# One small weight load of an attention and feed-forward kernel: the queue it is issued on, and how its second copy is made

## The chip, the cores and the metric

The kernel runs on one core of a Trainium2 chip. A core has five engines with instruction queues of their own: TensorE (matrix products, PE in the profile; PEld are its weight loads), VectorE (DVE), ScalarE (ACT), GpSimd (POOL) and SyncE (SP), which here only issues transfers. Transfers (DMAs) can be issued from SP, from ScalarE and from GpSimd, and are carried out by 16 DMA engines that the core has in common for all of them. The metric is the time of one execution on the device, in microseconds. Before the change the median of three runs is 282.02 us (280.19 to 282.04).

## The reference

Two layers follow each other. The first is a linear attention with a feature map of exponentials, over 8 batches of 8 heads, 576 tokens and 64 channels per head:

```python
def phi(x):
    proj = np.einsum('bhsd,df->bhsf', x, w_phi)          # w_phi: 64 x 128
    proj = proj - np.max(np.abs(proj), axis=-1, keepdims=True)
    return np.concatenate([np.exp(proj), np.exp(-proj)], axis=-1)
q_p, k_p = (phi(q), phi(k))
kv = np.einsum('bhsf,bhsd->bhfd', k_p, v)
z = np.sum(k_p, axis=2)
num = np.einsum('bhsf,bhfd->bhsd', q_p, kv)
den = np.einsum('bhsf,bhf->bhs', q_p, z)[..., None] + 1e-06
attn = (num / den)
```

The second takes the attention's result as 4608 tokens of 512 channels and computes `max(x @ w1, x @ w2, x @ w3) @ w_out`, with three 512 x 768 matrices and one of 768 x 512. The result is 4608 x 512 in float32.

## The kernel before

**Units and chunks.** The attention is done in 16 units of four heads each (`attention(u)`), the feed-forward layer in eight chunks of 512 tokens and a last one for the remaining 64 tokens of each batch (`chunk`). The chunks of the early batches run among the units of the later ones, so that all engines have work from both layers at the same time.

**One unit.** The queries and keys of a unit come in as bf16 `qk_bf`, most of them by transfers that GpSimd issues and that convert on the way (L439, L455). For unit 0 the keys come in float32 as `k_raw` in two halves, issued by SP (L449), and are converted on chip: the first half by VectorE, the second by GpSimd (L452). The last 64 queries of each head come as `q_tail` (L370) and are converted by GpSimd (L468). In the first four units TensorE transposes these tiles into PSUM (`tps`, L483) and VectorE or ScalarE copies them into `qkT` (L499, L501); later units use a transposing transfer (L508). In `qkT` two tokens' channels share the 128 rows: rows 0 to 63 belong to the even tile, rows 64 to 127 to the odd one. Then the projections follow: `psk` and `psq` (L536), `pst` for the tails (L557) and `psm` with the roles exchanged (L631). Each of them uses 64 of the 128 rows, once the upper and once the lower ones, and so w_phi must stand in both halves of the rows: that is the tile `wph` (bf16, 128 x 128). VectorE takes the maxima of the projections (L525), ScalarE the exponentials (L522, L582), GpSimd multiplies the values by exponentials (`vab`, L590), TensorE makes the products `kvps` (L611) and `psn` (L663), VectorE and GpSimd divide (L666 to L673), and the result is transposed into `xT`.

**Loading w_phi.** One transfer reads w_phi twice and fills all 128 rows of the float32 tile `wphi_f` (L400). SP issues it, between the two halves of the first keys. One VectorE instruction then converts `wphi_f` to `wph` (L408). Every projection of every unit depends on this conversion; the first of them is `psk` of unit 0.

**The order of the work.** Nothing is scheduled by the compiler: each piece of work is a `node`, with the engines that may run it and its assumed cost, and the long text PLAN gives for each node its number, engine (T TensorE, D VectorE, A ScalarE, G GpSimd, S SP), the numbers of the buffers that it opens, and a start time. `plan` (L246) reads the text. The instructions of each engine are emitted in the order of these starts; each engine works through its own list in order and waits at an instruction until what it needs is there. The start times are not enforced on the chip. The nodes that matter below are: 1 the constant tile for fillers, 2 the load of w_phi, 3 its conversion, 6 and 8 the two loads of the first keys, 7 and 9 their conversions, 10 and 180 loads of tails, 11 the first load of v, 13, 17 and 15 the first transposes, 14 ScalarE's copy of the first of them, 23 the first `psk`, 64 the first `psm`, 1546 ScalarE's load of its function table.

**Fillers.** Where PLAN leaves TensorE a gap early in the kernel, `fill` (L264 to L285) puts products of a constant tile in (`idler`, L866), whose results nobody reads. For each TensorE node it looks at the gap to the end of the one before. If the gap is over 0.35 us it emits a filler at 0.1 us after that end (at the very beginning at 0.65, when the constant tile is ready), and further ones in steps of 0.43 us while the time is up to 4.6 us, then of 0.26, as long as the time stays below the node's start less 0.8 us (less 0.2 us once it is past 4.6). Each needs a free PSUM bank. With the starts of before this gives 14 fillers, seven of them ahead of node 13 and none between nodes 13 and 23.

Of the kernel before, what the change touches and what calls it, by code (L numbers as in the profile page):

```python
# [8 lines left out]
FP32 = mybir.dt.float32  # L9
# [7 lines left out]
DF = 128  # L17
# [69 lines left out]
19T0@7.9 99G@7.9 1150G@8.1 333S0@8.3 34A@8.3 20D@8.4 21T1@8.5 31D@8.7 66A@8.8 1148G@8.9 68A@9.3 36D@9.3 40T06@9.5  # L87
38A@9.8 22D@9.9 41D@10.2 65A@10.3 43T4100@10.3 50A0@10.8 32D@10.8 47A@11.0 51G0@11.1 37A@11.2 102T0@11.3 42D@11.4
44A@11.7 69T52@11.9 35A@12.0 103D1@12.1 52G@12.2 71A@12.5 49D@12.7 123T103@12.8 72A@13.0 46D@13.0 53G@13.3 124D@13.4
54A@13.5 256G0@13.5 48A@13.7 100T6@13.8 125D@14.0 57A@14.0 70A@14.1 104T7@14.3 1149G@14.3 58T001@14.5 101D@14.6  # L90
73A@14.6 45A@15.1 113T53@15.1 56G@15.1 105D@15.2 106T2611@15.3 60A@15.4 59A@15.5 115D@15.6 116T74@15.6 74A0@15.7
126T1011@15.8 110A@15.9 114D@16.2 55G@16.2 128A@16.3 120A@16.6 119D@16.8 111A@17.1 183G@17.3 109D@17.4 61T53@17.5
255G@17.5 121A@17.6 112D@18.0 117A@18.1 332G1@18.3 63A@18.6 122D@18.6 133A0@18.7 75T63@18.9 62A@18.9 118A@19.1
135G0@19.1 132D@19.2 184T5@19.2 129D@19.5 107A@19.6 78T47@19.7 76D0@19.9 137A@20.1 134G@20.2 108A@20.3 185D0@20.3
188T6@20.5 189A@20.8 79D@20.9 147T2511@21.1 136A@21.1 127A@21.2 140G@21.3 77D@21.3 186T6@21.4 130A@21.5 405G3@21.5
331G@21.8 80D@21.8 149A@21.8 83T14@21.9 187D@22.2 131A@22.3 141T137@22.3 335G@22.5 148A@22.6 139G@22.8 84D1@22.8
197T060@23.0 142A@23.2 81D0@23.2 1159T2@23.3 150A@23.3 198D@23.4 157A1@23.8 138G@23.9 86T31@23.9 151A@24.0 199D@24.0
1161T6@24.2 143A@24.5 87D@24.6 1160A0@24.7 1157T7@24.8 259G@25.0 85D@25.1 82G0@25.2 88D@25.5 144T30@25.5 1162A@25.6
1158D@25.9 207T12@26.1 152T45@26.3 402G@26.4 146A@26.5 209D@26.6 145A@26.6 161T67@26.7 155A@26.8 158T03@27.0 89D0@27.2
154A@27.3 162D0@27.3 1169T2@27.3 90G@27.5 159D@27.8 153A@27.9 181D0@28.2 163D@28.3 156A@28.4 182S@28.4 160D@28.7  # L100
403G@28.7 224T0400@28.7 1170A@28.9 166T57@29.1 164D0@29.3 169T63@29.4 228A@29.4 165G1@29.6 167D1@29.6 1167T2@29.7
226A@29.9 208D@30.1 225A@30.5 170D@30.7 1153G@30.8 93T5@31.0 168D@31.1 1168A@31.3 91T6@31.3 171D@31.5 200T7011@31.7
227A@31.8 92D@31.9 190T12@32.0 205A@32.3 174T3@32.3 172D0@32.3 196D@32.5 1163T64@32.6 192A@32.7 173G@32.9 94D@33.1
202A@33.2 175D@33.5 195A@33.7 260T5@33.9 257D@33.9 206D@34.0 1151G@34.1 258S@34.2 191A@34.2 176T4@34.4 261D1@34.6
1165T3@34.7 1164A@34.7 194A@35.2 193D@35.3 201A@35.7 177D@35.9 210T1211@36.1 204A@36.1 1152G@36.2 266T16500@36.3
203D@36.3 1173T4@36.6 214A@36.6 272D@36.9 215A@37.1 264T7@37.5 216D@37.5 1183T0@37.6 270A@37.7 213D@37.9 268A@38.1
1174D0@38.2 1156G@38.3 1181T2@38.4 212A@38.6 269D@38.8 217A0@38.9 265A@39.1 1177T4@39.3 1166D@39.4 211A@39.4 267A@39.7
1184D@40.0 271A@40.2 286T3100@40.3 219G0@40.4 276T67@40.5 1178D@40.6 1182A@40.7 1193T0@40.8 287A@41.2 292D@41.2
234A1@41.4 282D@41.6 277A@41.6 262T2@41.7 1175T4@42.1 220A@42.1 1194D@42.2 288A@42.2 218G@42.5 278A@42.5 289D@42.8
1195T0@43.0 291A@43.0 263D@43.1 281A@43.3 279D@43.8 1179T5@43.9 280A@43.9 336S2@44.0 1196D@44.4 290A@44.4 1155G@44.6  # L110
1176A@44.7 300T7611@44.8 1180D@45.0 273T12@45.1 221T103@45.3 301A@45.3 274D@45.6 293A0@45.8 302A@46.0 275D@46.2
296A1@46.5 283T15@46.5 304A@46.6 294G@46.7 229T74@46.7 285D@47.0 1191T2@47.0 222A@47.1 232A@47.4 284D@47.6 223A@47.8
1189T5@47.9 233A@48.1 1192D@48.2 303A@48.6 295G@48.7 238T43@48.8 474S1@48.9 1190D@49.0 230A@49.1 235T21@49.1
305T60@49.5 239D1@49.6 231A@49.7 1197T5@49.8 236D@50.1 406S1@50.2 309A@50.2 240D@50.5 246T74@50.7 1154G@50.8 308A@50.8
237D@50.9 243T23@51.1 247D0@51.3 306A@51.3 297T001@51.5 244D@51.7 307A@52.0 248D@52.2 310A1@52.4 245D@52.6
371T2600@52.7 376T47@52.9 241D0@53.0 1171G@53.1 249D1@53.2 372A@53.2 1185T3@53.2 298D@53.3 299A@53.6 374A@53.9
404S0@54.1 1187T1@54.1 472G1@54.1 1186D@54.3 373A@54.4 334S@54.7 250G1@54.8 375A@54.9 1205T0@55.0 1188D@55.2
475S1@55.3 380A@55.4 322T63@55.8 378A@55.9 609S0@55.9 242G@56.1 319T12@56.2 379A@56.3 323D0@56.4 1206T@56.5 377A@56.8
320D@56.8 324D@57.3 473G@57.3 321D@57.7 314T41@57.8 541G3@58.0 1207A0@58.0 337T13600@58.2 315D1@58.4 311T27@58.5
339A@58.7 325D0@58.8 253T0@58.9 326G0@59.1 312D@59.1 342A@59.2 1198T@59.2 316D@59.5 254A@59.7 313D@60.0 543G@60.3  # L120
343D@60.4 476G@60.5 357T7200@60.6 424T040@60.8 317D0@61.0 361A@61.0 1201T1@61.1 360D@61.1 318G@61.3 1199A1@61.3
425D@61.5 338A@61.8 1202T@62.0 363D@62.1 341A@62.3 426D@62.4 1493G@62.5 359A@62.8 340D@63.0 362A@63.1 251T0@63.3
540G@63.3 358A@63.4 327T2@63.6 1203A2@63.6 252D@63.8 329T3@63.9 328A@64.2 344T76@64.3 330D@64.4 354T01@64.5 477S0@64.7
347T45@64.7 346D@64.9 1223T3@65.1 348A@65.2 345D@65.5 349A@65.9 1213T2@65.9 353D@66.1 1224A1@66.3 350D@66.7
1215T7@66.8 351A@66.8 355D@67.3 364A0@67.4 1214A@67.6 1225T4@67.7 366G1@67.8 356D@67.9 352A@68.1 367A@68.6
407T6011@68.6 1216A@68.7 1226D@68.8 427T1511@68.9 417T23@69.1 431A@69.3 1235T7@69.4 413D@69.4 429A@69.6 365G@69.9
422A@69.9 433D@70.0 1221T4@70.3 428A@70.4 420D@70.4 1200S@70.4 432A@70.6 381A1@70.9 430D@71.0 1204S@71.0 419A@71.1
1217T5@71.1 423D@71.3 1208S@71.6 412A@71.6 410D@71.9 611G0@72.0 1227T1@72.0 418A@72.1 744S1@72.2 608G@72.2 1236D@72.5
1218A@72.6 1233T2@72.9 1494G@72.9 1222A@73.1 1228D@73.1 542S@73.4 421A@73.6 1229T7@73.7 1234D@74.0 544S2@74.1
434A0@74.1 411A@74.3 436G0@74.4 414T31@74.7 408A@74.8 1230D@74.9 446T0211@74.9 368T045@75.2 448A@75.4 415D@75.5  # L130
# [158 lines left out]
def kernel(  # L289
# [109 lines left out]
    def phi_load(n_):  # L399
        queue_of[n_.eng].dma_start(wphi_f, w_phi.unsqueeze(0).to_broadcast([2, D, DF]))  # L400
# [497 lines left out]
```

## Time and profile before

| | |
|---|---|
| median of three runs | 282.02 us (280.19 to 282.04) |
| the profiled execution | 282.44 us |
| its span | 280.6 us |
| TensorE busy | 268.6 us, 96% of the span, 3460 products |
| VectorE busy | 224.0 us, 80% |
| ScalarE busy | 197.7 us, 70% |
| GpSimd busy | 161.3 us, 57% |
| moved by DMA | 43.24 MB |

The span goes from the first to the last instruction that the profiler recorded; the time of the execution is 1.84 us longer. Times in the rows count from the start of the span. A row of the view in order of time gives the start, the duration, the engine, the line, the operation, what it writes and reads, how many instructions are merged into the row, and in brackets how long the engine stood idle before it and what it waited for. A row of the chain of waits gives the start, the duration and what the end of the kernel hung on during it. In the rows of DMA issues the last number is the time from issue to landing. The rows of a DMA queue give packets, MB and the time of their packets as a share of the 16 engines; q1 is SP's queue, q0 GpSimd's, q10 ScalarE's.

### The profile page before, as it was taken

Reading aid. Unit: us, or ns where it says so; the run is one execution under the profiler, and the core shown is the slowest. Engines: PE = TensorE matmul, PEld = TensorE weight load, DVE = VectorE, ACT = ScalarE, POOL = GpSimd, SP = SyncE. Lnnn points to the kernel's source line nnn. Section 1 sums busy time; section 2 is a strip of 40 time slices with the busy share of each in tenths; the row PEclk is TensorE's granted clock in tenths of the full one; section 3 lists DMA queues with packets and bytes.
Section 4 is the critical chain, followed back from the end, with each engine's and each line's share of the span. In section 5 each row is a group of like instructions: output and inputs, shape, how many; then the busy total and the mean of one; then the engine's idle time right before and its main releaser. Section 6 shows DMA issues by size and latency. Waiting matters only on the chain.

```text
span 280.6 us, 8449 instructions
## 1 busy us (share of the span) xinstructions
PE 268.6 (96%) x3460; PEld 150.2 (54%) x3460; DVE 224.0 (80%) x452; ACT 197.7 (70%) x488; POOL 161.3 (57%) x158
## 2 busy tenths in 40 slices
PE   5788999999999999999999999999999999999994
PEld 1457654765465546555564466445654664444451
DVE  1798999979988899998987999978998994375530
ACT  2699999988998999999376997689969850200001
POOL 6599899996795693666575483339345753000000
PEclk9997999999999999999999999999999999999998
DMA  7999999199999799997969979499444015200054
GB/s 146 238 236 208 208 247 199 34 304 168 227 187 191 140 201 267 194 189 88 224 100 233 181 127 242 65 252 174 96 85 161 2 24 147 77 0 0 2 146 153
DMA packets 70632, 43.24 MB, mean 154 GB/s; under 512 B 47042, under 2 KB 61762, under 8 KB 70594
## 3 DMA queue, kind: packets, MB, share of 16 engines
q1 hardware_dynamic: 55602, 30.91, 48.5%
q0 software_dynamic: 14912, 11.77, 28.7%
q8 instruction: 27, 0.44, 0.6%
q14 instruction: 11, 0.09, 0.1%
q10 hardware_dynamic: 80, 0.03, 0.0%
HBM read 34.67 MB, written 9.44 MB: 157 GB/s over the span
## 4 chain that ended last, share of the span: by engine, by line
PE 87%; DVE 4%; ACT 3%; DMA 2%; POOL 1%; issue 1%; SPq 0%; DVEq 0%
PE ups L713 34%; PE ops L746 17%; PE ops L741 11%; PE psn L663 7%; PE kvps L611 6%; PE psk L536 3%; PE psm L631 3%; PE psq L536 3%; DMA wphi_f<-in_w_phi_dram 2%; DVE m L525 2%; ACT Ek L522 1%; PE pst L557 1%; PE tps L483 1%; PE pxT L683 1%; POOL x_sb L673 1%
## 5 line engine op out<-in xcount | busy, mean ns | idle before, releaser
L713 PE MATMUL ups<-xT,w_bf 128*128 128x512 bf16 x432 | 100.7, 379 | 0.6 <-issue 0.5
L590 POOL TENSOR_TENSOR vab<-v_raw,em 128x1152 bf16<-128x1152 f32 (+1 forms) x36 | 67.9, 1903 | 22.3 <-ACT em L582 21.5
L522 ACT ACTIVATE Ek<-psk 128x512 bf16<-128x512 f32 x128 | 72.5, 625 | 5.0 <-PE psk L536 4.4
L522 ACT ACTIVATE Eq<-psm 128x512 bf16<-128x512 f32 x128 | 71.7, 626 | 4.5 <-PE psm L631 4.3
L713 PEld LDWEIGHTS <-w_bf 128*128 128x128 bf16 x432 | 39.4, 98 | 46.4 <-issue 2.3
L673 POOL TENSOR_TENSOR x_sb<-y,rden 128x640 bf16<-128x640 f32 x32 | 39.9, 1253 | 33.0 <-DVE rden L671 28.9
L746 PE MATMUL ops<-wout_bf,hT 128*128 128x512 bf16 (+2 forms) x222 | 51.4, 374 | 0.0
L721 ACT ACTIVATE hT<-ups 128x512 bf16<-128x512 f32 x34 | 20.6, 618 | 37.4 <-PE ups L713 37.4
L525 DVE TENSOR_REDUCE m<-psk 128x4 f32<-128x512 f32 x64 | 42.7, 681 | 3.3 <-PE psk L536 2.0
L719 DVE TENSOR_TENSOR hT<-hT,ups 128x512 bf16<-128x512 bf16 x54 | 36.0, 680 | 8.8 <-PE ups L713 8.0
L525 DVE TENSOR_REDUCE m<-psq 128x4 f32<-128x512 f32 x64 | 41.6, 679 | 0.7 <-PE psq L536 0.6
L666 DVE TENSOR_TENSOR y<-psn,sq 128x325 f32<-128x325 f32 x64 | 29.9, 486 | 3.4 <-PE psn L663 1.9
L746 PEld LDWEIGHTS <-hT 128*128 128x128 bf16 x222 | 20.4, 98 | 22.4 <-issue 0.3
L669 DVE TENSOR_TENSOR y<-y,psn 128x325 f32<-128x325 f32 x64 | 29.2, 485 | 1.0
L663 PEld LDWEIGHTS <-Eq 128*128 128x128 bf16 x512 | 23.3, 99 | 10.5 <-issue 1.8
L522 ACT ACTIVATE Et<-pst 128x256 bf16<-128x256 f32 x64 | 24.0, 409 | 3.0 <-PE pst L557 2.6
L663 PE MATMUL psn<-kv_sb,Eq 128*128 128x65 bf16 x512 | 25.2, 195 | 0.9 <-DVE m L525 0.6
L755 DVE COPY osb<-ops 128x512 f32<-128x512 f32 (+1 forms) x22 | 14.7, 669 | 12.7 <-PE ops L746 12.7
L741 PE MATMUL ops<-xT 128*128 128x512 bf16 x96 | 24.5, 379 | 0.0
L755 ACT COPY osb<-ops 128x512 f32<-128x512 f32 (+1 forms) x15 | 8.9, 593 | 20.8 <-PE ops L746 13.3
L536 PEld LDWEIGHTS <-qkT 64*128 64x128 bf16 x512 | 16.4, 96 | 11.6 <-issue 8.4
L611 PE MATMUL kvps<-vab,Ek 64*128 64x65 bf16 x1024 | 20.5, 191 | 0.7 <-POOL vab L590 0.7
(71 smaller groups left out, 313.5 us busy)
## 6 DMA issues: line engine op xcount, KB each, us to landing
v_raw<-in_v_dram SPq DMA_DIRECT2D x16, 576.0 KB, 6.8
out_dram<-osb SPq DMA_DIRECT2D x32, 256.0 KB, 3.8
qk_bf<-in_k_dram POOLq DMA_DIRECT2D x15, 288.0 KB, 7.4
qk_bf<-in_q_dram POOLq DMA_DIRECT2D x15, 256.0 KB, 7.8
w_bf<-in_moe_w_dram POOLq DMA_DIRECT2D x3, 768.0 KB, 19.1
q_tail<-in_q_dram SPq DMA_DIRECT2D x16, 64.0 KB, 6.1
wout_bf<-in_moe_w_out_dram POOLq DMA_DIRECT2D x1, 768.0 KB, 15.6
out_dram<-osb SPq DMA_DIRECT2D x6, 128.0 KB, 2.4
```

The costliest lines, as they stand in the source:

```text
L522: nc.scalar.activation(out, ps, EXP, scale=1.0 - 2.0 * s)
L525: nc.vector.tensor_reduce(out, ps, AXX, ALU.max, apply_absolute_value=True)
L536: nc.tensor.matmul(pss[par]()[:, i, :], lhsT=qkT()[r, block(c, h * HB + i), :], rhs=wph[r, :], start=True, stop=True)
L590: made.append(any_of(n_, lambda n_, g=g, t0=t0, t1=t1: (nc.vector if n_.eng == "DVE" else nc.gpsimd).tensor_tensor(vab()[:, g, t0:t1, 0:D] ...
L611: nc.tensor.matmul(kvps[ab]()[:, pr, g, :], lhsT=Ek[g]()[r, t, :] if t < MT else Et[g]()[r, 0, t - MT, :], rhs=vab()[r, g, t, :], start=(p ...
L663: nc.tensor.matmul(psn[g]()[:, c, :], lhsT=Eq[g]()[:, t0:t0 + P] if c < 4 else Et[g]()[:, 1, pr, :], rhs=kv()[:, pr, ab, g, :], start=True ...
L666: n_ = nd("xu", {"DVE": 0.42}, lambda pr=pr, ab=ab, psn=psn, y=y: nc.vector.tensor_tensor(y()[:, ab], psn[0](), sq()[:, 2 * pr + ab, :].un ...
L673: divs.append([any_of(n_, lambda n_, pr=pr, y=y, rden=rden: (nc.vector if n_.eng == "DVE" else nc.gpsimd).tensor_tensor(x_sb()[:, pr].rear ...
L713: nc.tensor.matmul(ups(), lhsT=w_bf[i + 1][:, ct, j * P:(j + 1) * P], rhs=tokens_of(ct), start=(ct == 0), stop=(ct == CT - 1))
L719: nc.vector.tensor_tensor(hT()[:, j, :], hT()[:, j, :], ups(), ALU.max)
L741: nc.tensor.matmul(ops_()[:, 0:width], lhsT=tile_of(ct, tt), rhs=line_w[c_i > MOVE][:, ct, cols], start=(ct == 0), stop=False)
L746: nc.tensor.matmul(ops_()[:, 0:width], lhsT=hT()[:, j, tt * P:(tt + 1) * P], rhs=wout_bf[:, j, cols], start=False, stop=(j == JT - 1))
```

## The change

The tile `wphi_f` has 64 rows instead of 128, and the transfer reads w_phi once, without a broadcast. ScalarE issues it, ahead of its table load; SP's list loses it, so the second half of the first keys follows the first half directly. VectorE converts `wphi_f` twice, once into rows 0 to 63 of `wph` and once into rows 64 to 127, as one node. PLAN is written anew: the order of the nodes on VectorE, GpSimd and TensorE stays the same as before, on SP and ScalarE it differs in the moved load alone. The starts differ by some tenths of a microsecond, and PSUM bank numbers are in part others. Of 920 buffer openings 23 follow another earlier user than before. The fillers follow from the new starts.

```diff
 PLAN = """
-1D@0.3 1546A@0.7 6S0@0.7 4G0@1.2 2S@1.3 8S@1.9 5G@2.0 10S0@2.5 95G1@2.7 7D@3.4 0G@3.5 11S0@3.8 96G@4.0 13T0@4.2
-180S1@4.4 14A0@4.6 179G2@4.8 3D@4.8 23T00100@5.3 9G@5.5 29D@5.8 24A@5.8 17T2@5.9 178G@6.1 15T3@6.3 18D@6.4 25A@6.4
-97D@6.7 16D@6.8 64T2400@6.9 1147G@6.9 28A@6.9 98S@7.0 26D@7.1 33T35@7.3 67A@7.4 30T67@7.5 12G@7.7 39D@7.8 27A@7.9
...
+1D@0.3 2A@0.7 6S0@0.7 4G0@1.2 1546A@1.3 8S@1.3 10S0@1.9 5G@2.0 95G1@2.7 11S0@3.2 0G@3.5 7D@3.8 180S1@3.8 96G@4.0
+3D@4.3 13T0@4.5 179G2@4.8 14A0@5.0 9G@5.5 23T00100@5.6 17T2@5.9 29D@6.1 24A@6.1 178G@6.1 15T3@6.3 18D@6.7 25A@6.7
+1147G@6.9 97D@7.0 16D@7.1 64T2400@7.2 28A@7.2 98S@7.3 26D@7.5 33T35@7.6 12G@7.7 67A@7.7 30T67@7.9 99G@7.9 39D@8.1
+1150G@8.1 27A@8.2 19T0@8.2 333S0@8.3 34A@8.7 20D@8.7 21T1@8.8 1148G@8.9 31D@9.1 66A@9.1 68A@9.6 36D@9.7 40T06@9.8
...
-    wphi_f = const.tile([P, DF], FP32, name="wphi_f")
+    wphi_f = const.tile([D, DF], FP32, name="wphi_f")
...
     def phi_load(n_):
-        queue_of[n_.eng].dma_start(wphi_f, w_phi.unsqueeze(0).to_broadcast([2, D, DF]))
+        queue_of[n_.eng].dma_start(wphi_f, w_phi)
+
+    def phi_cast():
+        for r in (slice(0, D), slice(D, P)):
+            nc.vector.tensor_copy(wph[r, :], wphi_f)
...
-    n_phi = node("phi", 0, {"SP": 0.6, "ACT": 0.6}, None, [], [], pipe=0.32, lat=2.0, packet=40.0)
+    n_phi = node("phi", 0, {"ACT": 0.6}, None, [], [], pipe=0.32, lat=2.0, packet=40.0)
     n_phi.fn = lambda n_=n_phi: phi_load(n_)
-    n_phi = node("phi", 0, {"DVE": 0.25}, lambda: nc.vector.tensor_copy(wph, wphi_f), [n_phi], [])
+    n_phi = node("phi", 0, {"DVE": 0.45}, phi_cast, [n_phi], [])
```

More of the change, by code (lines that the diff above doesn't have):

```diff
@@ L89 @@
[L89 to L128, printed above, removed]
@@ L240 @@
+1488S@275.2
 """
```

264 lines of the change are left out of this document (151 added, 113 removed).

## The prediction

> **What bounds the kernel now.** I read the page's forty slices first, then the chain of waits, then the start in order of time, because the change touches one load in the first 8 us.
>
> ```profile
> span 280.6 us, 8449 instructions
> PE   5788999999999999999999999999999999999994
> PE 87%; DVE 4%; ACT 3%; DMA 2%; POOL 1%; issue 1%; SPq 0%; DVEq 0%
> 14.00:21.00 7.00, 5.75 (x125) 3.91 (x126) 7.00 (x14) 6.97 (x24) 6.53 (x9) 1.00 1.19 237
> 28.00:56.00 28.00, 27.76 (x435) 16.90 (x433) 27.07 (x58) 27.24 (x69) 26.93 (x18) 1.00 0.95 172
> ```
>
> The last two rows are stretches of the span: busy time of PE, PEld, DVE, ACT and POOL, then granted clock, DMA share and GB/s. From 28 us on TensorE has work for nearly every microsecond, and 87% of the chain is TensorE. So whatever the start gains or loses is handed on to the end, as long as the other engines keep the same distance. Between 14 and 21 us VectorE and ScalarE are full and TensorE waits for them. What comes before that is latency:
>
> ```profile
> 0.74 0.39 SPq L449 DMA_DIRECT2D k_raw<-in_k_dram  x1
> 0.74 1.28 ACT L847 ACT_TABLE_LOAD   x1 [0.74 <-PEq L882]
> 1.06 3.17 PE L866 MATMUL idler<-idle 128*128 128x512 bf16 x7 [1.06 <-DVE idle L405]
> 1.19 0.71 SPq L400 DMA_DIRECT2D wphi_f<-in_w_phi_dram  x1
> 1.95 0.43 SPq L449 DMA_DIRECT2D k_raw<-in_k_dram  x1
> 3.60 0.55 DVE L452 CAST qk_bf<-k_raw 128x576 bf16<-128x576 f32 x1 [2.60 <-DMA k_raw<-in_k_dram]
> 4.37 0.58 PE L483 MATMUL tps<-ident,qk_bf 128*128 128x128 bf16 x4
> 4.99 0.58 ACT L499 COPY qkT<-tps 128x512 bf16<-128x512 bf16 x1 [2.97 <-PE tps L483]
> 7.21 0.23 DVE L408 CAST wph<-wphi_f 128x128 bf16<-128x128 f32 x1 [3.07 <-DMA wphi_f<-in_w_phi_dram]
> 7.59 0.61 PE L536 MATMUL psk<-wph,qkT 64*128 64x128 bf16 x8 [2.63 <-DVE wph L408]
> 8.24 0.69 DVE L525 TENSOR_REDUCE m<-psk 128x4 f32<-128x512 f32 x1 [0.80 <-PE psk L536]
> 8.42 0.66 POOL L452 CAST qk_bf<-k_raw 128x576 bf16<-128x576 f32 x1 [2.74 <-DMA k_raw<-in_k_dram]
> ```
>
> The first projection (psk, 7.59) has its keys transposed and copied at 4.99 + 0.58 = 5.57, but waits for w_phi, which was issued at 1.19 and landed at 7.19. That is the one DMA on the chain (2% of it). GpSimd also waits, until 8.42, for the second half of the first keys, which SP issued right behind w_phi.
>
> **The change part by part.** *The load.* The old one has 128 rows on SP's queue, between the two key halves. The new one has 64, from ScalarE's queue at 0.74. Loads to compare, with KB (the two key halves and v by their issue windows) and us to landing:
>
> ```profile
> k_raw<-in_k_dram SPq DMA_DIRECT2D x1, 288.0 KB, 2.8
> k_raw<-in_k_dram SPq DMA_DIRECT2D x1, 288.0 KB, 6.4
> wphi_f<-in_w_phi_dram SPq DMA_DIRECT2D x1, 64.0 KB
> q_tail<-in_q_dram SPq DMA_DIRECT2D x1, 64.0 KB, 7.0
> v_raw<-in_v_dram SPq DMA_DIRECT2D x1, 576.0 KB, 9.8
> out_dram<-osb ACTq DMA_DIRECT2D x1, 32.0 KB, 1.9
> 3.00:3.50 0.50, 0.50 (x2) 0.15 (x1) 0.00 (x0) 0.00 (x0) 0.50 (x1) 1.00 0.36 70
> ```
>
> The first key half, 288 KB, needed 2.8 us; w_phi with 64 KB needed 6.0. So w_phi is not slow by its bytes. In the last row, the half microsecond in which the first key half ends, the DMA engines are busy only 0.36 and move 70 GB/s, although w_phi and the second half have been issued by 2.38; in the stretch from 14 to 21 us, quoted above, they move 237 GB/s. I read this as w_phi trickling and holding what stands behind it. The new load is bounded by 1.9 us (the 32 KB store on ScalarE's queue) and 7.0 us (the 64-row tail load, in the crowd): it lands between 2.64 and 7.74. I take 2.8, the key half issued at the same moment: 3.5 us.
>
> The Trainium skill, "DMA: Bandwidth & Descriptors", section "Why a DMA increments its semaphore by 16 and not by 1", says that the number of DMA engines is the largest up to 16 that divides the outermost dimension of both sides; by it the broadcast (outermost 2) used two engines and the plain load uses sixteen. The trace gives no count by engine, but the slow 64 KB beside the fast 288 KB agree.
>
> *ScalarE.* It issues for 0.71 us (SP's row) ahead of its table load, which then ends at 0.74 + 0.71 + 1.28 = 2.73. Its first use is the copy at 4.99, so this costs nothing, with 2.3 us to spare.
>
> *VectorE.* Two conversions for one. A 64-row one takes between half of 0.23 and all of it, so the step costs 0.23 to 0.46; I take 0.46. They follow the key cast: 3.60 + 0.55 + 0.46 = 4.61, a microsecond before the copied keys at 5.57, so the second conversion is hidden. If w_phi landed last it would add 0.23.
>
> *TensorE's filler products.* `fill` derives them from the written starts. Before the first transposes it now emits eight (0.65, then steps of 0.43, below 4.5 - 0.8) instead of seven. Between them and psk it emits three (4.83, 5.09, 5.35, below 5.6 - 0.2), where there were none: with the old starts the loop began at 4.53 and its limit was 5.3 - 0.8 = 4.5. The one between psk and the next transposes goes, and one more comes ahead of psm. What one takes of the chain while TensorE is slow:
>
> ```profile
> 9.74 0.43 PE idler L866
> ```
>
> 0.43 each. Eight from 1.06 end at 4.5; the four transposes start there (before: 4.37) and stream a quarter of a filler's columns each, 0.43 in all, to 4.94; ScalarE has copied by about 5.7; three fillers end at 4.94 + 1.29 = 6.23. So psk starts at 6.2 instead of 7.59: **1.4 us** earlier. Without fillers it would be 1.9; they eat 0.5.
>
> *The stretch behind psk.* The chain of waits there, and VectorE's part of it:
>
> ```profile
> 7.59 0.61 PE psk L536 x8
> 8.20 0.54 PE idler L866
> 62.20 0.33 PE psk L536 x8
> 9.20 0.42 DVE L499 COPY qkT<-tps 128x512 bf16<-128x512 bf16 x1 [0.27 <-PE tps L483]
> 11.21 0.69 DVE L525 TENSOR_REDUCE m<-psk 128x4 f32<-128x512 f32 x1 [0.40 <-PE psk L536]
> 12.14 0.42 DVE L499 COPY qkT<-tps 128x512 bf16<-128x512 bf16 x1 [0.24 <-PE tps L483]
> ```
>
> From 8.24 to 12.14 VectorE idles 0.27 + 0.40 + 0.24 = 0.91 us for TensorE, which carries a filler there and runs at half pace (psk x8 0.61, later in the kernel 0.33). The transposes of the second key half wait for GpSimd's cast (8.42 to 9.08). Now the filler is gone, TensorE no longer pauses 2.63 us before psk and so may run fast sooner, and the second half is issued at 1.19. Bounds: none of the 0.91 comes back, or all: 1.4 to 2.3 in all at 12.14. I take 2.1, because the filler alone is 0.54 of it.
>
> *What is late next.* The second key half: issued at 1.19, it lands between 1.19 + 2.8 = 4.0 and 1.19 + 6.4 = 7.6. GpSimd is free from about 5.7 (the end of its issues in the fourth row below). At 7.6 the gain at these transposes would be 0.8; I take about 5, nearer the first half, since nothing stands before it. The first half of the queries (first two rows: issued at 1.24, 5.0 to landing) lands at 6.24 and is wanted behind psk, from 6.6 on: no stall, but little room. The first values are next:
>
> ```profile
> 1.24 2.37 POOL L439 DMA_DIRECT2D qk_bf<-in_q_dram  x3 [0.80 <-POOLq L882]
> qk_bf<-in_q_dram POOLq DMA_DIRECT2D x1, 128.0 KB, 5.0
> 3.83 0.65 SPq L364 DMA_DIRECT2D v_raw<-in_v_dram  x1
> 4.24 1.44 POOL L455 DMA_DIRECT2D qk_bf<-in_k_dram  x2
> 14.46 2.26 POOL L590 TENSOR_TENSOR vab<-v_raw,em 128x576 bf16<-128x576 f32 x2 [1.55 <-ACT em L582]
> 23.00:24.00 1.00, 1.00 (x18) 1.00 (x15) 0.96 (x3) 1.00 (x5) 1.00 (x2) 0.50 1.25 209
> 24.46 0.61 PE psm L631 x2
> 27.25 0.27 PE psq L536 x8
> ```
>
> The values were issued at 3.83 and landed 9.8 later (13.6), used at 14.46; they too are now issued 0.7 earlier and behind no broadcast. If they only gained that 0.7, the product could start at 12.9, a gain of 1.5. GpSimd moves its next issues (weights) up by some 2 us with its cast; they queue behind its own earlier loads, so I give them no cost. The plan keeps the order on every engine, apart from the moved load; other PSUM bank numbers change which buffer some products follow, for which I take 0, between -0.3 and +0.3 (two waits the size of the 0.27 above).
>
> *Sum.* 2.1 us less on the profiled execution: 282.44 - 2.1 = 280.3 (a span of 278.5 and the 1.84 around it). That execution is 0.42 over the median of the runs, 282.02, so the forecast is **279.9 us**; 1.2 to 2.8 of gain gives its own range, 279.2 to 280.8.
>
> **The rivals.**
>
> *The held queue stays slow.* If the second key half or the values land as slowly as now, only their earlier issue counts: 0.76 us (1.95 - 1.19), so 281.3. For it: the DMA share is 1.19 even at 14 to 21 us, so the crowd remains. Against it: the 0.36 right where the key half should flow.
>
> *Only the issue time is saved.* The load keeps its 6.0 us: it lands at 6.74 and psk starts 0.2 earlier (0.45 - 0.23): 281.8. This is what the change would be if it did not do what it says. The Trainium skill, "DMA: Bandwidth & Descriptors", section "Issuing engines are not separate DMA queues", says that starting from several engines saves only issue time; by that rule alone, this is the result. Against it stands that half the rows go too.
>
> *The clock.* In the row at 23 us TensorE has half the granted clock with 1.00 busy, after a thin stretch; it pays from 24.46 to 27.25, where it is on the chain, until the clock returns (0.80 in the following row):
>
> ```profile
> 26.00:27.00 1.00, 1.00 (x43) 0.93 (x42) 0.93 (x2) 0.74 (x2) 1.00 (x3) 0.80 1.20 225
> ```
>
> Half clock thus lasts some 3.4 us (23.0 to 26.4), of which 1.9 are on the chain and cost 1.0. A faster start shifts this. It may fall away: 1.0 more, 278.9. Or a second such piece falls where TensorE sets the pace: 1.7 less gained, 281.6.
>
> *Slower: the load is late on its new queue.* If ScalarE's row is served like the tail load, 7.0 us, w_phi lands at 7.74, two conversions and psk's 0.15 follow: 8.37 instead of 7.59, 0.8 slower: 282.8. It decides from a landing after 7.19 - 0.23 = 6.96. Against it: at 0.74 nothing stands in the queues but the key half.
>
> **How the numbers follow.** Chances: forecast 0.58; clock piece gone 0.14; second clock piece 0.08; queue stays slow 0.10; issue time only 0.06; late load 0.04. A difference of 1% is 2.8 us, about what a measurement of this kernel can tell from no change (its three runs spread over 1.85). The limit for faster is thus 279.2: all of the clock case and a tenth of the forecast, 0.20. Slower by 1% would need 284.8, which no case reaches; I leave 0.03 for what I haven't seen, and 0.77 for within 1%. The range goes from 278.5 (clock piece gone, with part of the forecast's upper bound) to 281.9 (issue time only).
>
> **What would show it.** Right: the cast of w_phi starts at about 4.2, behind the key cast and not behind a DMA; eight and three fillers; psk at about 6.2; GpSimd's key cast before 7; VectorE's third copy of keys and queries at about 10 instead of 12.14; no engine waits for v_raw; 28 to 56 us as full as before. Wrong: a VectorE wait for wphi_f beyond 5.6, a GpSimd wait for k_raw until 8, a granted clock of 0.50 over more or other stretches, or TensorE gaps behind 28 us that were not there.

## The result, and the profile after

| | before | after |
|---|---|---|
| median of 20 runs each, side by side | 282.15 us (279.23 to 287.31) | 280.04 us (277.89 to 281.57) |
| the profiled execution | 282.44 us, span 280.6 | 279.17 us, span 277.1 |

The ratio of the changed kernel to the one before is 0.994, with a 95% interval from 0.9911 to 0.9968, or 1.7 us; the medians differ by 2.1 us. The ratio leaves out executions in a slower state, and so it isn't that of the medians. A second comparison, made along with the experiments below, gave 0.9884 (0.9848 to 0.992), where 0.990 to 0.996 had been expected. Single executions of one kernel spread over 4 to 8 us, so the pair of profiled executions, which lie 3.3 us apart, shows the mechanism and not the size.

The page of the kernel after, its span, TensorE's forty slices, the granted clock, the chain by engine, and ScalarE's queue:

```profile
span 277.1 us, 8459 instructions
PE   8889999999998999999999999999999999999993
PEclk9899999999999999999999999999999999999999
PE 92%; ACT 4%; DVE 2%; issue 0%
q10 hardware_dynamic: 160, 0.07, 0.1%
```

The first slices were 5788 and are 8889, the DMA share of the chain (2%) is gone, and TensorE's part of the chain went from 87% to 92%. The start of the kernel after, in order of time:

```profile
0.74 0.54 ACTq L400 DMA_DIRECT2D wphi_f<-in_w_phi_dram  x1
0.73 0.87 SPq L453 DMA_DIRECT2D k_raw<-in_k_dram  x2
1.06 3.60 PE L870 MATMUL idler<-idle 128*128 128x512 bf16 x8 [1.06 <-DVE idle L409]
4.06 0.55 DVE L404 CAST wph<-wphi_f 64x128 bf16<-64x128 f32 x2
4.75 0.81 PE L870 MATMUL idler<-idle 128*128 128x512 bf16 x3
4.95 0.58 ACT L503 COPY qkT<-tps 128x512 bf16<-128x512 bf16 x1 [2.35 <-PE tps L487]
5.59 0.40 PE L540 MATMUL psk<-wph,qkT 64*128 64x128 bf16 x8
5.67 0.68 POOL L456 CAST qk_bf<-k_raw 128x576 bf16<-128x576 f32 x1
8.64 0.41 DVE L503 COPY qkT<-tps 128x512 bf16<-128x512 bf16 x1
11.39 2.26 POOL L594 TENSOR_TENSOR vab<-v_raw,em 128x576 bf16<-128x576 f32 x2 [1.55 <-ACT em L586]
22.65 0.68 DVE L503 COPY qkT<-tps 128x1024 bf16<-128x1024 bf16 x1
269.56 0.69 DVE L759 COPY osb<-ops 128x512 f32<-128x512 f32 x1 [0.60 <-PE ops L750]
```

No instruction in these rows waits for w_phi or for the second key half any more. psk starts at 5.59 instead of 7.59, GpSimd's key conversion at 5.67 instead of 8.42, VectorE's third copy at 8.64 instead of 12.14, the first products of the values at 11.39 instead of 14.46. The last two rows are a late copy of the start and VectorE's last copy. Their counterparts in the kernel before, from the same view:

```profile
26.07 0.69 DVE L499 COPY qkT<-tps 128x1024 bf16<-128x1024 bf16 x1 [0.49 <-PE tps L483]
272.99 0.69 DVE L755 COPY osb<-ops 128x512 f32<-128x512 f32 x1 [0.60 <-PE ops L746]
```

3.42 us earlier at the first, 3.43 at the last: in this pair of executions all was won before 26 us and none of it lost in the 247 us that follow. Windows of the kernel after, with the columns of the prediction (busy time of PE, PEld, DVE, ACT, POOL, granted clock, DMA share, GB/s):

```profile
3.00:3.50 0.50, 0.50 (x2) 0.15 (x1) 0.00 (x0) 0.00 (x0) 0.50 (x1) 1.00 0.98 367
11.00:15.00 4.00, 3.91 (x30) 1.97 (x30) 3.58 (x8) 4.00 (x15) 3.61 (x5) 0.57 1.19 258
23.00:24.00 1.00, 1.00 (x46) 0.90 (x39) 1.00 (x4) 1.00 (x4) 1.00 (x3) 1.00 1.24 217
28.00:56.00 28.00, 28.00 (x399) 16.04 (x398) 26.29 (x57) 26.76 (x68) 27.89 (x17) 1.00 1.00 197
```

Where the DMA engines moved 70 GB/s at 3.0 to 3.5 us they now move 367. At 23 us the clock is full; a half-clock piece lies at 11 to 15 instead, where the mean of 0.57 over 4 us makes 2 x 0.43 x 4 = 3.4 us of it (half clock over a part of a window takes half of that part from the mean). From 28 us on TensorE is full, as before.

### The profile page after: what moved, and what is told of

Its sections match the earlier page's. It is cut to its first block, busy times and chain, and to the rows that moved or that the text cites. A ratio compares the mean times of both kernels' runs of the same rounds, so it can differ in the third digit from the quotient of the medians.

```text
span 277.1 us, 8459 instructions
## 1 busy us (share of the span) xinstructions
PE 267.7 (97%) x3464; PEld 149.1 (54%) x3464; DVE 223.6 (81%) x453; ACT 197.4 (71%) x488; POOL 161.3 (58%) x158
## 4 chain that ended last, share of the span: by engine, by line
PE 92%; ACT 4%; DVE 2%; issue 0%
PE ups L717 34%; PE ops L750 17%; PE ops L745 11%; PE psn L667 7%; PE kvps L615 6%; PE psk L540 3%; PE psm L635 3%; PE psq L540 3%; PE idler L870 2%; PE pm L820 2%; ACT Ek L526 2%; DVE m L529 1%; PE pxT L687 1%; PE pst L561 1%; PE tps L487 1%; ACT Eq L526 1%
## 5 line engine op out<-in xcount | busy, mean ns | idle before, releaser
L526 ACT ACTIVATE Et<-pst 128x256 bf16<-128x256 f32 x64 | 24.6, 420 | 3.0 <-PE pst L561 2.6
L759 DVE COPY osb<-ops 128x512 f32<-128x512 f32 (+1 forms) x22 | 14.7, 666 | 12.7 <-PE ops L750 12.7
```

Source lines behind the costliest of these rows:

```text
L526: nc.scalar.activation(out, ps, EXP, scale=1.0 - 2.0 * s)
```

## The experiments

Two questions were open after the result. Which part of the change brings the earlier start: the form of the load (64 rows, no broadcast), its place (no longer between the key halves), or the rewritten plan with its fillers? And does what is gained at the start reach the end? The table has the numbers of all kernels; "copy" is the one that stood at 26.07 in the kernel before, and "pauses" is the sum of TensorE's pieces of "issue" on the chain of waits between 78 and 96 us, which come up further below.

| kernel | psk | GpSimd's key conversion | copy | pauses | last copy | median us | ratio to before (95%) |
|---|---|---|---|---|---|---|---|
| before | 7.59 | 8.42 | 26.07 | 0.55 | 272.99 | | 1 |
| changed | 5.59 | 5.67 | 22.65 | 0.77 | 269.56 | 280.04 | 0.994 (0.9911 to 0.9968) |
| changed, again | 6.29 | 5.76 | 23.07 | 0.86 | 269.46 | 279.68 | 0.9884 (0.9848 to 0.992) |
| broadcast on ScalarE | 6.66 | 5.74 | 23.77 | 1.61 | 271.45 | 280.06 | 0.9901 (0.9864 to 0.9939) |
| two plain loads | 6.67 | 5.75 | 23.75 | 1.35 | 271.03 | 280.88 | 0.9889 (0.9849 to 0.9928) |
| plain, SP, old plan | 5.48 | 7.01 | 25.60 | 2.12 | 274.38 | 282.4 | 0.9981 (0.995 to 1.0012) |
| the same, again | 5.60 | 6.91 | 25.46 | 2.13 | 273.54 | 282.0 | 0.9986 (0.995 to 1.0022) |
| plain, SP, new plan | 5.75 | 6.99 | 23.39 | 1.41 | 270.85 | 280.24 | 0.9941 (0.9906 to 0.9976) |
| plain, SP behind the keys | 5.54 | 5.67 | 22.68 | 1.81 | 270.51 | 281.28 | 0.9936 (0.9893 to 0.9979) |
| change, old plan | 5.69 | 5.76 | 24.21 | 0.89 | 270.56 | 279.95 | 0.9902 (0.9867 to 0.9937) |
| old load, new plan | 6.54 | 7.15 | 23.92 | 2.29 | 271.85 | 281.45 | 0.9926 (0.9895 to 0.9957) |
| before with fillers | 7.44 | 7.91 | 25.01 | 0.31 | 270.72 | 281.14 | 0.9944 (0.9907 to 0.998) |
| no fillers before psk | 5.75 | 5.68 | 24.68 | 0.60 | 271.05 | 280.18 | 0.9874 (0.9827 to 0.9921) |
| no late fillers | 5.46 | 5.70 | 23.38 | 1.09 | 270.31 | 280.61 | 0.9949 (0.9916 to 0.9982) |

The times in the first columns are of one profiled execution each. The runs of before that were shared by the kernels of one comparison had medians of 282.48 to 283.46.

### The form: the broadcast on the new queue, and two plain loads

The first kernel is the changed one, but with the old transfer of 128 rows and the one conversion:

```diff
-    wphi_f = const.tile([D, DF], FP32, name="wphi_f")
+    wphi_f = const.tile([P, DF], FP32, name="wphi_f")
...
-        queue_of[n_.eng].dma_start(wphi_f, w_phi)
+        queue_of[n_.eng].dma_start(wphi_f, w_phi.unsqueeze(0).to_broadcast([2, D, DF]))
...
-        for r in (slice(0, D), slice(D, P)):
-            nc.vector.tensor_copy(wph[r, :], wphi_f)
+        nc.vector.tensor_copy(wph, wphi_f)
```

> The plan of the changed kernel, but the load is the old broadcast of 128 rows (64 KB), issued on ScalarE's queue at 0.74, with one conversion. Theory (the broadcast itself is slow, on whichever queue, and holds only what stands behind it in its own row): it again takes about 6 us and lands at about 6.7, psk starts at about 7.1 instead of 5.59; the second key half on SP's queue has nothing before it and lands at about 4.5 as in the changed kernel, GpSimd casts it at 5.7. Time between the two: some 1 us under the kernel before. Rival (it was the place in SP's row that was slow): lands by 4, psk at 5.6, time as the changed kernel, 2 us under before. Second rival (a slow load holds both queues, since descriptors are made in one place): the second key half lands at 7 or later.

The second fills the 128 rows by two plain transfers on ScalarE's queue and converts them at once:

```diff
-        queue_of[n_.eng].dma_start(wphi_f, w_phi)
+        for r in (slice(0, D), slice(D, P)):
+            queue_of[n_.eng].dma_start(wphi_f[r, :], w_phi)
```

> The plan of the changed kernel; all 128 rows come from HBM, by two plain loads of 64 rows from ScalarE's queue, and one conversion makes the bf16 tile. Theory (the form of the broadcast was the cost, not its rows or bytes): both land by 4.5, psk at 5.6, time as the changed kernel within 0.5 us. Rival (the rows count): the second load lands at 6 or later, psk at 6.4 or later, time 0.5 to 1 us above the changed kernel.

The rows of ScalarE's queue in the first 8 us (packets, MB, share of the engines' time), changed kernel:

```profile
q10 hardware_dynamic: 80, 0.03, 1.5%
```

Broadcast on ScalarE, the same row:

```profile
q10 hardware_dynamic: 130, 0.07, 2.7%
```

The same kernel in order of time, the conversion that waits for this transfer and the first projection:

```profile
6.02 0.49 DVE L403 CAST wph<-wphi_f 128x128 bf16<-128x128 f32 x1 [1.83 <-DMA wphi_f<-in_w_phi_dram]
6.66 0.40 PE L539 MATMUL psk<-wph,qkT 64*128 64x128 bf16 x8 [0.34 <-DVE wph L403]
```

Two plain loads, the row of the queue:

```profile
q10 hardware_dynamic: 160, 0.07, 3.4%
```

and the conversion in order of time:

```profile
5.81 0.72 DVE L404 CAST wph<-wphi_f 128x128 bf16<-128x128 f32 x1 [1.60 <-DMA wphi_f<-in_w_phi_dram]
```

The plain load has 64 packets of rows and 16 more, the two plain ones 128 and 32, the broadcast 128 and 2. So the broadcast ended on 2 engines and each plain load on 16, which is what the Trainium skill, "DMA: Bandwidth & Descriptors", section "Why a DMA increments its semaphore by 16 and not by 1", states for an outermost dimension of 2 against 64. With the broadcast w_phi is converted from 6.02 instead of 4.06, and psk starts 0.4 to 1.1 us later than in the two profiles of the changed kernel.

The two plain loads are hardly better, though each has 16 engines: they are converted from 5.81, and psk starts at 6.67. Their times from issue to landing:

```profile
DMA to landing us min/median/max: 3.2/3.8/4.4
```

The first lands as fast as the one load of the changed kernel (3.1). The second, issued at 1.3, needs 4.4: 14 packets of ScalarE's queue still fall between 4.5 and 5.0 us, where GpSimd's queue has 95.4% of the engines' time. The expectation for this kernel (both by 4.5, psk at 5.6) failed, and its rival, that the rows count (psk at 6.4 or later), came true at the start. So the broadcast is not shown to be slower than 128 rows in two plain loads: both are late, and in both a good part of the rows goes out behind 3.5 us, beside GpSimd's transfers.

The second key half comes as early as in the changed kernel in both (5.74 and 5.75), and the time is not measurably another: 0.9901 and 0.9889 beside 0.9884 in the second comparison. For the broadcast on ScalarE some 1 us under before had been expected; 0.9901 is 2.8.

### The place: the plain load on SP

The kernel before, its plan untouched, with the plain load and two conversions; SP still issues it between the key halves:

```diff
-    wphi_f = const.tile([P, DF], FP32, name="wphi_f")
+    wphi_f = const.tile([D, DF], FP32, name="wphi_f")
...
-        queue_of[n_.eng].dma_start(wphi_f, w_phi.unsqueeze(0).to_broadcast([2, D, DF]))
+        queue_of[n_.eng].dma_start(wphi_f, w_phi)
+
+    def phi_cast():
+        for r in (slice(0, D), slice(D, P)):
+            nc.vector.tensor_copy(wph[r, :], wphi_f)
...
-    n_phi = node("phi", 0, {"DVE": 0.25}, lambda: nc.vector.tensor_copy(wph, wphi_f), [n_phi], [])
+    n_phi = node("phi", 0, {"DVE": 0.25}, phi_cast, [n_phi], [])
```

> The plan of the kernel before, so the load stays between the key halves on SP's queue, but it is the plain one of 64 rows with two conversions. Theory (shape): it takes about 3 us, lands at about 4.3, the second key half lands at about 5 instead of 8.4, psk starts at about 5.7; time 1.5 to 2 us under before, close to the changed kernel. Rival (the queue is what counts): lands at about 7 as before, time as before within 0.5 us.

Since it gave almost nothing (0.9981), it was run again, together with the same load under the plan of the changed kernel:

> The plain load on SP's queue with the plan of before, once more: the first time psk came at 5.48 and yet the time was only 0.5 us under before, with three stretches of half clock before 28 us in the profiled execution. Theory A (the second key half, held to 7.0 by the load ahead of it, thins TensorE's start, and the clock drops in most executions): 0.995 to 1.000 of before, again two or three half-clock stretches before 28 us. Theory B (that was one unlucky draw): 0.988 to 0.993, one stretch.

```diff
-1D@0.3 2A@0.7 6S0@0.7 4G0@1.2 1546A@1.3 8S@1.3 10S0@1.9 5G@2.0
+1D@0.3 6S0@0.7 4G0@1.2 2S@1.25 1546A@1.3 8S@1.3 10S0@1.9 5G@2.0
...
-    n_phi = node("phi", 0, {"ACT": 0.6}, None, [], [], pipe=0.32, lat=2.0, packet=40.0)
+    n_phi = node("phi", 0, {"SP": 0.6}, None, [], [], pipe=0.32, lat=2.0, packet=40.0)
```

> The changed kernel, but its plain load stays on SP's queue between the key halves; plan and fillers are those of the changed kernel. Theory (both parts count: the second key half comes to GpSimd at 7 instead of 5.7, but the fillers keep TensorE's pace): psk at 5.6, GpSimd's key cast at about 7.0, time 0.5 to 1.5 us above the changed kernel, 0.990 to 0.994 of before. Rival (the key half alone decides): 0.997 or more, as with the old plan. Second rival (pace alone decides): as the changed kernel, 0.986 to 0.989.

The last of this group tells the queue from the place in it: SP issues the plain load, but behind both key halves (`8S@1.3 2S@1.35`), with the same line for `n_phi`.

> The plan of the changed kernel and its plain load, but issued by SP, behind the second half of the first keys instead of ahead of it. Theory of place: what SP's queue costs is that the second key half goes out third, after w_phi (GpSimd's conversion of it at 6.99 with the same plan and the load in between). With the half right behind the first it lands as in the changed kernel and GpSimd converts it before 6.0; w_phi, issued at about 1.8, lands by 5.2, psk starts at 5.7 to 6.3, and the time is that of the changed kernel, a ratio of 0.984 to 0.992. Theory of the queue: whatever order SP issues in, w_phi and the half share its queue and the later of the two pays: w_phi lands after 6.0, psk starts at 6.7 or later, and the ratio is 0.993 to 0.999, like the load between the halves (0.9941).

Plain load on SP under the old plan, in order of time:

```profile
4.35 0.72 DVE L404 CAST wph<-wphi_f 64x128 bf16<-64x128 f32 x2
5.48 0.40 PE L540 MATMUL psk<-wph,qkT 64*128 64x128 bf16 x8 [0.68 <-ACT qkT L503]
7.01 0.66 POOL L456 CAST qk_bf<-k_raw 128x576 bf16<-128x576 f32 x1 [1.25 <-DMA k_raw<-in_k_dram]
```

Its DMA queues from 3.0 to 3.5 us (packets, MB, share of the 16 engines' time; q0 is GpSimd's, q1 SP's):

```profile
q0 software_dynamic: 19, 0.01, 59.3%
q1 hardware_dynamic: 50, 0.03, 20.3%
```

and the same half microsecond among its windows:

```profile
3.00:3.50 0.50, 0.50 (x2) 0.15 (x1) 0.00 (x0) 0.00 (x0) 0.50 (x1) 1.00 0.80 84
```

The changed kernel, SP's queue in the same half microsecond:

```profile
q1 hardware_dynamic: 79, 0.18, 93.3%
```

The load behind the keys on SP, in order of time:

```profile
5.18 0.55 DVE L404 CAST wph<-wphi_f 64x128 bf16<-64x128 f32 x2 [1.04 <-DMA wphi_f<-in_w_phi_dram]
5.67 0.68 POOL L456 CAST qk_bf<-k_raw 128x576 bf16<-128x576 f32 x1
22.68 0.69 DVE L503 COPY qkT<-tps 128x1024 bf16<-128x1024 bf16 x1
```

and its half microsecond:

```profile
3.00:3.50 0.50, 0.50 (x2) 0.15 (x1) 0.00 (x0) 0.00 (x0) 0.50 (x1) 1.00 1.00 364
```

With the plain load between the halves w_phi itself is early (psk at 5.48), yet the second half is still late, and the dip at 3.0 us is still there: 84 GB/s. In that half microsecond GpSimd's queue, with the queries that convert on the way, holds 59.3% of the engines' time with 19 packets. In the changed kernel it has no packet there yet, and the second half has the engines (79 packets, 93.3%). This holds in all profiles: where w_phi stands between the halves, GpSimd's queue has 15 to 43 packets between 3.0 and 3.5 us, and where it doesn't, none. The half is issued at 1.80 in the one case and directly behind the first, with it from 0.73 to 1.60, in the other, and that turn decides: either it flows ahead of GpSimd's packets or it is mixed with them.

What such a packet costs is not settled. 0.593 x 0.5 x 16 / 19 makes 0.25 us each here; the kernel before has, in the same half microsecond,

```profile
q0 software_dynamic: 19, 0.01, 17.5%
```

0.07 us each, with the engines busy for 0.36 of the time only, and its second half is later still. So full engines are not the whole reason.

Behind the keys, still on SP, the second half and the late copy are as in the changed kernel, to 0.03 us at the copy (22.68 and 22.65), although w_phi is converted at 5.18 instead of 4.06 and psk takes 0.64. So at the start it is the place that counts, and the queue doesn't. That the mixing is what delays the half is read from these rows; no run took GpSimd's queries away.

In the time, the place shows under the old plan: 0.9981 and 0.9986 with the load between the halves, 0.9902 with the load moved (next section), with intervals that don't meet. Under the new plan it doesn't show: between the halves 0.9941, behind them 0.9936. The theory of the place had asked for at most 0.992 there, that of the queue for at least 0.993; the interval covers both, and a part of the answer lies far behind the start, in the pauses below.

### The plan and its fillers

The change with the old plan, in which only the load moved (14 fillers and the bank numbers of before):

```diff
-1D@0.3 1546A@0.7 6S0@0.7 4G0@1.2 2S@1.3 8S@1.9 5G@2.0
+1D@0.3 2A@0.7 1546A@0.7 6S0@0.7 4G0@1.2 8S@1.9 5G@2.0
...
```

> The load, its queue and the two conversions of the changed kernel, but the plan of before in which only the load's entry is moved: starts, fillers (14) and PSUM bank numbers are the old ones. Theory (the load is the cause, the plan's other edits are not): psk at about 5.6, GpSimd's key cast at 5.7, third copy near 10.5 at slow pace as without the three fillers; time 1.5 to 3 us under before, within 1 us of the changed kernel. Rival (new bank numbers and fillers carry the gain; the plain load on SP's queue with the old plan brought almost none): time within 0.7 us of before.

The old load between the key halves, with the new plan:

```diff
-1D@0.3 2A@0.7 6S0@0.7 4G0@1.2 1546A@1.3 8S@1.3 10S0@1.9 5G@2.0
+1D@0.3 6S0@0.7 4G0@1.2 2S@1.25 1546A@1.3 8S@1.3 10S0@1.9 5G@2.0
...
```

> The kernel before in its load (128 rows by broadcast, on SP's queue between the key halves, one conversion), with the plan of the changed kernel: its starts, its 18 fillers, its bank numbers. Theory (the load is the cause): w_phi lands at about 7.2, psk at 7.5, time within 0.7 us of before. Rival (the plan is the cause): time 2 us or more under before.

The kernel before with eight more fillers while it waits for w_phi, in `fill`:

```diff
+        if n.kind == "T" and n.start == 4.2:
+            todo += [(4.3 + 0.01 * i, make(1 + i % 3)) for i in range(8)]
         free = n.start + n.costs["PE"]
```

> The kernel before, with eight filler products between the first transposes and the first psk, where TensorE stood idle for 2.63 us; nothing else. Theory (part of the gain is TensorE's pace, not w_phi's landing): psk starts at about 7.5 as before, but takes 0.40 instead of 0.61, and VectorE's third copy at L499 comes at 11.2 to 11.6 instead of 12.14; time 0.5 to 1 us under before. Rival (pace does not matter here, since VectorE and ScalarE are full): third copy at 12.0 or later, time as before within 0.3 us.

The changed kernel without the three fillers between the first transposes and psk:

```diff
+    quiet = False
...
+        if quiet:
+            free, quiet = n.start, False
+        if n.kind == "T" and n.start == 4.5:
+            quiet = True
         gap, t = n.start - free, max(free + 0.1, ready)
```

> The changed kernel without the three filler products between the first transposes and the first psk. The prediction held them for a cost of 0.5 us. Theory now (they ran at 0.22 each, and bridge TensorE's pause so that it keeps the fast pace): psk still starts at about 5.55, but TensorE pauses 0.6 us; whether its pace drops shows in psk x8 (0.40 fast, 0.61 slow) and in VectorE's third copy at L503 (8.64 in the changed kernel): up to 9.3 if the pace drops, time up to 0.7 us above the changed kernel. Rival (fillers cost 0.5 us or do nothing): third copy at 8.6 or earlier, time equal or 0.5 us less.

And without the five fillers behind 10 us, where the chain of the changed kernel runs over them:

```diff
+    todo = [x for x in todo if not (x[0] > 10.0 and x[1].__name__ == "filler")]
     return [fn for _, fn in sorted(todo, key=lambda x: x[0])]
...
-        def fn():
+        def filler():
...
-        return fn
+        return filler
```

> The changed kernel without its fillers behind 10 us (five of 18). In the first profile of the changed kernel three of them stood on the chain at half clock, 1.5 us together. Theory (they only cost): 0.5 to 1.5 us under the changed kernel, 0.983 to 0.987 of before. Rival (they keep the clock up until 28 us): further stretches of half clock before 28 us, time 0.5 us or more above the changed kernel, 0.990 or more of before.

Before with fillers, in order of time: psk is nearly as late as ever (7.44 and 7.59), but it takes 0.40 where it took 0.61, and the third copy comes at 10.61 instead of 12.14.

```profile
4.75 2.75 PE L868 MATMUL idler<-idle 128*128 128x512 bf16 x8
7.44 0.40 PE L538 MATMUL psk<-wph,qkT 64*128 64x128 bf16 x8
10.61 0.41 DVE L501 COPY qkT<-tps 128x512 bf16<-128x512 bf16 x1
```

No fillers before psk: the load and the keys are early, but psk starts at TensorE's slow pace and the third copy, at 8.64 and 9.50 in the two profiles of the changed kernel, comes 1.9 and 1.1 us later.

```profile
5.75 0.61 PE L545 MATMUL psk<-wph,qkT 64*128 64x128 bf16 x8 [0.68 <-ACT qkT L508]
10.56 0.42 DVE L508 COPY qkT<-tps 128x512 bf16<-128x512 bf16 x1
```

Old load with the new plan: psk runs at the fast pace, but late, and the second key half comes at 7.15 although the broadcast stands ahead of it.

```profile
6.54 0.40 PE L536 MATMUL psk<-wph,qkT 64*128 64x128 bf16 x8 [0.55 <-DVE wph L408]
7.15 0.66 POOL L452 CAST qk_bf<-k_raw 128x576 bf16<-128x576 f32 x1 [1.47 <-DMA k_raw<-in_k_dram]
```

The chain of waits of the changed kernel, where it runs over fillers:

```profile
4.91 0.66 PE idler L870 x3
12.37 0.96 PE idler L870 x2
13.88 0.54 PE idler L870
```

A window of the kernel without the late ones:

```profile
11.00:18.00 7.00, 6.07 (x94) 4.71 (x94) 5.83 (x12) 6.20 (x22) 6.65 (x9) 0.51 1.22 238
```

Fillers alone are worth something measurable: 0.9944 with nothing else changed, and 0.9926 for the whole new plan with the old load, 2.1 us by the ratio, as the rival (the plan is the cause) had it. The change under the old plan gives 0.9902, 2.8 us, as the theory of the load had it; both together give 0.9884. The parts overlap rather than add up (0.7% and 1.0% alone, 1.2% together in the second comparison). The single fillers can't be told apart by the time: without the three the ratio is 0.9874, though in that profile the copy comes 1.6 us later than in the changed kernel's second one (24.68 and 23.07). Three of the late ones hold 0.96 + 0.54 = 1.5 us of the chain, and leaving them out gained nothing (0.9949): in its profile the granted clock is 0.51 over 7 us, so 2 x 0.49 x 7 = 6.9 us at half clock, twice the 3.4 of the changed kernel. My expectation that they only cost something has fallen. No kernel here is measurably faster than the changed one.

### What reaches the end

The chain of waits between 78 and 96 us, its longest piece in which nothing is shown to be waited for. The kernel before:

```profile
85.12 0.55 issue
```

The changed kernel:

```profile
86.86 0.77 issue
```

Plain load on SP under the old plan:

```profile
91.64 1.88 issue
```

The same kernel, run again:

```profile
90.80 1.87 issue
```

The load behind the keys on SP:

```profile
87.28 1.68 issue
```

In these pieces TensorE stands and waits for nothing that the profile shows, in the midst of work that keeps it full. They take from the lead: behind the keys on SP the copy is 26.07 - 22.68 = 3.39 us ahead of before and the last copy 272.99 - 270.51 = 2.48. The changed kernel, with the same start and 1.04 less of pauses, keeps 3.43. Over all fourteen profiles the stretch from the copy to the last copy takes 245.7 to 246.9 us where the pauses are under 1 us together, and 246.9 to 248.8 where they are more.

The plain load on SP under the old plan was 0.47 and 0.61 ahead at the copy, and 1.39 and 0.55 behind at the end. So its ratios of 0.998 have more than one cause. It gains little at the start, and both of its profiles show three pieces at half clock there, as theory A of its second run expected: from 7 to 28 us the mean granted clock is 0.76, which makes 2 x 0.24 x 21 = 10 us at half clock, where before and the changed kernel have 0.92 and the same load under the new plan 1.00. And its pauses are 1.6 us longer than before. The two profiles of that kernel have the same long pause to 0.01 us. The two of the changed kernel have 0.77 and 0.86 in all, but at other places: all of it at 86.86 in the first, 0.65 of it at 80.96 in the second. As far as two pairs tell, the sum goes with the program rather than with the execution.

The traces point to a cause. Between 70 and 100 us the fourteen profiles have 18 such pauses of 0.2 us or more, and every one of them ends 1.3 to 1.7 us after the end of a transfer of 16 KB of instructions. In the changed kernel that transfer runs from 85.34 to 86.29 and TensorE goes on at 87.62; in the plain load on SP under the old plan it runs from 91.10 to 92.08, and TensorE goes on at 93.52. Not every such transfer has a pause behind it. So it looks as if TensorE waits there for instructions that come late; no run tested it.

## Why the prediction was right, and where its steps were off

The forecast of 2.1 us and 279.9 us was met by the medians (2.1, 280.04). That it was met so closely is luck. The ratio of the same comparison, 0.994, is 1.7 us; the second comparison, 0.9884 of 282.85, is 3.3 us, and the two profiled executions lie 3.3 us apart, both more than the own range of the forecast (1.2 to 2.8) allowed. In the profiled pair the sum of the steps was too small: 3.5 us at the third copy and 3.4 at the end, where 2.1 were taken. The direction and the path (w_phi off the chain, the second half early, TensorE without its pause) were right; these are the steps one by one.

**The new load.** Forecast: landed at 3.5, converted at about 4.2 behind the key conversion. Measured: 3.1 us to landing, so at 3.8, converted at 4.06. Right.

**ScalarE** paid nothing for the issue (0.54 us instead of 0.71): its first copy stands at 4.95, before at 4.99. **VectorE's step** took 0.55 for two conversions, one behind the other (0.30 and 0.22), hidden as forecast.

**The fillers** came out as eight and three. "They eat 0.5" took 0.43 each, TensorE's slow pace. In the second profile they ran so, and psk started at 6.29, as forecast. In the first they ran at 0.22 (three in 0.66 on the chain). What differs is the moment at which the pace turns from half to full: 4.6 us in the first, 7.0 in the second, though TensorE had worked without a pause since 1.06 in both (the granted clock in the rows is 1.00 all the while). So the price of this step depends on the execution. Whether the three are a cost or a gain by themselves the times don't tell: 0.9874 without them, 0.9884 with them. A like pause bridged in the kernel before was worth 0.6%.

**psk** at 6.2: measured 5.59 and 6.29. The size was right, within the pace.

**Behind psk.** Forecast 1.4 to 2.3 us, taken 2.1, third copy at about 10. Measured 3.5 us, 8.64 (9.50 in the second profile: 2.6). Of the 3.5, 2.0 are there at psk already and 1.5 come behind it (1.3 and 1.3 in the second profile), where the bound allowed 0.91. It counted only the idle times of VectorE that its rows name. Where VectorE's instructions follow each other without a pause they also overlap a little (its first maximum ends at 6.05 + 0.69 = 6.74, the copy behind it starts at 6.70), and in the first profile psk takes 0.40 instead of 0.61. This is the term that was sized too low.

**The second key half** lands before 5.67, where GpSimd takes it without a wait; forecast about 5. Right in time and wrong in its reason. "W_phi trickling and holding what stands behind it" is not needed for the delay: the plain load, left in its place, doesn't trickle (3.1 us to landing) and the half is late all the same (7.01, 6.91, 6.99). Behind the broadcast in its old place the half was converted at 8.42, 7.91 and 7.15. So the form explains at most a part of the delay, and the place more than a microsecond of it (6.99 against 5.67 with the same load, queue and plan).

**The rivals.** "The held queue stays slow" (281.3) and "only the issue time is saved" (281.8) are out by the 367 GB/s and by w_phi's 3.1 us. As to the rule that stands behind the second, the Trainium skill, "DMA: Bandwidth & Descriptors", section "Issuing engines are not separate DMA queues": the load behind the keys on SP agrees with it, since which engine issued the load made no difference to the second key half (5.67) and to the late copy; what the rule leaves out is the order of issue, and that moved the second key half. **The clock**: both halves of this rival happened at once. The half-clock piece at 23 us is gone, and one lies at 11.3 to 14.7 instead, where VectorE waits 0.42 us for a projection. From the third copy to the copy at 26.07 the lead goes from 3.50 to 3.42: the two nearly cancel. **The late load** didn't happen.

**The first queries and values.** For the queries no stall was forecast; TensorE waited 0.28 us for them, at 6.26. No engine waited for the values, as forecast: their first products started at 11.39 behind ScalarE's exponentials, earlier than the 12.9 of the forecast.

**Changed bank numbers**, costed at nothing, weren't tested by themselves. **28 us and behind** is as full as before, as forecast, but for the pauses, which the prediction knew nothing of.

## What to carry to other kernels

When two transfers of a queue are both urgent, a small one between them costs the second its turn (here its conversion came at 7.0 instead of 5.7): look at which transfer of another queue gets in between, in the half microsecond where the first ends. Where the small one still lands before it is used, it can go behind the large one, on whichever queue. In the time, moving it out showed under the old plan (1.0%); under the new plan its place on SP didn't. And the pace of TensorE at the start is a quantity of its own: bridging a pause of 2.6 us with products whose results nobody reads gave 0.6% here, beside 1.0% for the moved load under the old plan.

## What the runs showed that was not expected

**Pauses of TensorE at 80 to 92 us** of 0.3 to 2.3 us in all, by program, as told above: large enough to hide or to feign a difference of half a per cent between kernels whose starts are equal.

**Half-clock pieces of 3.4 us**, one or two or three before 28 us, at another place in nearly every profile; two of the fourteen have none. By the Trainium skill, "TensorE: Matmul & The Clock Gate", section "What's actually happening", the clock is set by windows of 3413 ns that run freely; the 3.4 us of the changed kernel and the 6.9 of the one without late fillers agree with one and two of them. The turn of the pace at the start fits the same windows: it lies 3 x 3.41 us before the end of the piece in the changed kernel (4.6 and 14.8), 4 x 3.41 without the late fillers (4.3 and 18.0) and 2 x 3.41 in the change under the old plan (9.2 and 16.0). So where the windows happen to lie seems to decide how long an execution starts at half pace; no run could set it.

**The conversion of w_phi** varies threefold: two of 64 rows took 0.55 us together in the changed kernel and 0.72 in the plain load on SP under the old plan; one of 128 rows took 0.23 in the kernel before, and 0.72 with two plain loads and 0.49 with the broadcast on ScalarE, where GpSimd's conversion of the keys (0.68 us from 5.75 and 5.74) ran beside it. That the two share something would fit these rows, but not the plain load on SP: its slow conversion (0.47 of the 0.72) had only GpSimd's issues beside it. The cause is open.
